# The experts' two layers as plain float32 products, the second one computed transposed and turned back

## The chip, the core and the metric

One core of one Trainium2 chip. The metric is device time in microseconds (us) from the start to the end of one launch of the kernel, median over several runs. PE is TensorE, DVE VectorE, ACT ScalarE, POOL GpSimd, SP the engine that issues most DMAs.

## What is computed

Three layers follow one another: a masked attention, a dense two-layer MLP with squared ReLU, and a mixture of eight experts. Only the last is touched:

```
def _moe2_ref(x, w_gate, w1, w2):          # N, D, E, F = 1536, 512, 8, 1024
    cap = N // E                           # 192 tokens for each expert
    logits = x @ w_gate
    order = np.argsort(-flat)              # best (token, expert) pairs first
    ...
    for e in range(E):
        mask = assigned == e
        h = np.maximum(x[mask] @ w1[e], 0.0)
        out[mask] = h @ w2[e]
```

In the part left out, the pairs are taken in this order, and a token goes to the first expert that still has room. Inputs and output are float32. The experts' weights are 8 x 2 x 512 x 1024 numbers, 33.5 MB.

## The kernel before

The whole program is written as operations with an engine, an estimated duration, a priority and dependencies; a planner (`Sched`) simulates the engines with these estimates, and the instructions are emitted in the order that comes out. So each engine's queue has a fixed order, and a wait in it holds up all that stands behind it. Buffers and PSUM banks are resources that an operation takes (`acq`) and gives back (`rel`). PSUM has two double banks (`S0`, `S1`) and four single ones (`TP0`, `TP1`, `m`, `O`, together called "B").

Attention and the MLP come first. Then the router and the experts run side by side. The **router** finds which expert fills first, then the next, in eight phases; each is a long chain of small DVE operations with a few PE steps: comparisons of all tokens' values (L1345, one for each tile of 128 tokens, 12, then 9, then 6 tiles), counts by PE (L1352), a transposition and a minimum (L1397 to L1409), places of the chosen tokens (L1143, L1146, L1421), their slots (L1465, L1471, L1475). A phase gives an expert's number `ei` and the indices `ix` of its 192 tokens. The next phase needs the tokens that are left.

For each **expert** `p`, POOL gathers the 192 tokens by an indirect DMA (L1652), PE turns them (L1668, L1669), and ACT and DVE write them as two parts, high and low, each rounded to float32r (L1672, L1676). float32r is the type that PE takes in one pass, with fewer bits of the mantissa. The weights come in four groups `g` of 256 hidden features, 1 MB each (L1614, L1615, two DMAs of 512 KB). Each group is split as well: ACT writes the high parts (L1618, two instructions), POOL and in part DVE the low parts, raw minus high (L1622, two instructions; `DVE_LO` tells which are DVE's). There are four raw places and five split ones.

First layer: for each group, two halves `j` of 128 features, four chunks `c` of 128 inputs. One product with the high weights on high and low tokens (L1707, 384 columns), one with the low weights on the high tokens (L1708, 192 columns). ACT and DVE add the two sums, apply ReLU and split the result again (L1711, L1715, L1718, L1723). Second layer: tokens are the stationary operand, w2 the moving one with 512 columns; per group and half, three products for tokens 0 to 127 (L1752 to L1754) and two for the other 64 (L1757 or L1760, L1758). The sums over all groups stay in a double bank, then ACT and DVE copy them (L1782, L1785, L1788), and POOL scatters the rows to the output (L1793). The last expert's results lie in two single banks.

`keep` (L1079) fills gaps of PE with products of no use (L1082) until the first expert's first product.

## Time and profile before

| | us |
|---|---|
| median of three runs | 909.86 (907.74 to 917.37) |
| span of the profiled execution | 906.2 |
| PE, DVE, ACT, POOL busy | 787.5, 770.8, 505.1, 579.2 |
| bytes moved by DMA | 113.21 MB |

The span runs from the first to the last instruction of one execution; it lies 3.7 us under the median. Busy times are sums over the span. Idle time is put down to the releaser, the instruction whose end let the engine go on. PE records are pipelined: a record's duration contains the way through the array, so the rate of a series is read from the distance of the starts. PEclk is the clock granted to the array (1 is full speed). In a timeline row the first number is the start in us, the second the duration, and `xN` says that N records of one kind stand in it.

### The profile page before, as it was taken

The page shows a single profiled execution, that of the slowest core. Times are in us where ns is not written, and L with a number is a line of the kernel's source. Part 1 is how long each engine was busy: PE and PEld are TensorE (multiplying, and loading weights), DVE is VectorE, ACT ScalarE, POOL GpSimd, SP SyncE. Part 2 cuts the span into 40 slices and gives each one's busy share as a digit, 9 for nine tenths or more (in the row PEclk, how much of TensorE's full clock was granted, in tenths as well). Part 3 has the DMA queues.
Part 4 walks back from the last instruction along what each step waited for, and adds up shares of the span by engine and source line. Part 5 has one row for each costly group of instructions (what it writes and reads, how often), then busy time and mean ns, then how long its engine had stood idle before and what let it go on. Part 6 is the DMA issues. An engine that isn't in the chain of part 4 may idle for free. (4 is left out here: it accounts for less than half of the span.)

```text
span 906.2 us, 14120 instructions
## 1 busy us (share of the span) xinstructions
PE 787.5 (87%) x4879; PEld 667.4 (74%) x4879; DVE 770.8 (85%) x1288; ACT 505.1 (56%) x943; POOL 579.2 (64%) x468
## 2 busy tenths in 40 slices
PE   8999999999779989989787876997787685888977
PEld 5797889889668878877676765984667474667866
DVE  6898999999987898998999998278898897986772
ACT  7898999999665535434433232454354343434642
POOL 3687787778775766755445454585566564567762
PEclk9999999999999999999899898988798796978999
DMA  8955856575122354333422220013442451645531
GB/s 201 234 127 125 180 128 143 120 162 125 47 94 97 137 185 140 129 117 125 163 93 94 91 94 1 12 60 107 144 157 75 147 177 60 214 149 169 204 134 35
DMA packets 99878, 113.21 MB, mean 125 GB/s; under 512 B 42560, under 2 KB 75712, under 8 KB 99808
## 3 DMA queue, kind: packets, MB, share of 16 engines
q1 hardware_dynamic: 97760, 106.03, 40.5%
q0 software_dynamic: 2048, 6.29, 2.1%
q8 instruction: 38, 0.62, 0.3%
q14 instruction: 32, 0.26, 0.1%
HBM read 82.42 MB, written 6.29 MB: 98 GB/s over the span
## 5 line engine op out<-in xcount | busy, mean ns | idle before, releaser
L1622 POOL TENSOR_TENSOR rf<-ff,rf 128x1024 fp32r<-128x1024 f32 x54 | 132.1, 2466 | 53.7 <-ACT rf L1618 53.4
L575 POOL TENSOR_TENSOR f<-f 128x768 f32<-128x768 f32 x96 | 144.8, 1512 | 32.0 <-PE psTP L583 13.2
L796 POOL TENSOR_TENSOR r<-f,r 128x384 fp32r<-128x384 f32 x64 | 85.7, 1341 | 99.1 <-ACT r L794 98.9
L773 POOL TENSOR_TENSOR r<-f,r 128x1024 fp32r<-128x1024 f32 x32 | 92.7, 2896 | 30.3 <-ACT r L771 25.7
L810 PE MATMUL psS<-r 128*128 128x512 f32 x384 | 100.2, 405 | 5.6 <-DVE f L820 4.6
L794 ACT ACTIVATE r<-f 128x384 fp32r<-128x384 f32 x64 | 33.3, 524 | 125.7 <-DVE f L792 125.7
L1707 PE MATMUL psS<-rf,rf 128*128 128x384 f32 x256 | 91.0, 409 | 10.8 <-DVE ff L1715 8.4
L563 DVE TENSOR_REDUCE f<-psS 128x1 f32<-128x768 f32 x96 | 90.5, 945 | 4.7 <-PE psS L547 3.1
L566 ACT ACTIVATE f<-psS,f 128x768 f32<-128x768 f32 x96 | 86.9, 906 | 3.9 <-POOL f L575 1.8
L547 PE MATMUL psS<-r 128*128 128x384 f32 x384 | 87.9, 350 | 0.8 <-ACT f L566 0.8
L810 PEld LDWEIGHTS psS<-r 128*128 128x128 f32 x384 | 73.3, 194 | 19.8 <-DVE f L820 4.9
L783 PE MATMUL psO<-r 128*128 128x384 f32 x408 | 80.5, 344 | 7.3 <-DVE f L792 7.3
L783 PE MATMUL psTP<-r 128*128 128x384 f32 x336 | 67.4, 349 | 19.0 <-DVE f L792 18.7
L783 PEld LDWEIGHTS psO<-r 128*128 128x128 f32 x408 | 73.1, 193 | 11.2 <-DVE f L792 10.7
L783 PEld LDWEIGHTS psTP<-r 128*128 128x128 f32 x336 | 59.9, 193 | 26.3 <-DVE f L792 24.9
L1618 ACT ACTIVATE rf<-ff 128x1024 fp32r<-128x1024 f32 x64 | 65.8, 1047 | 10.7 <-issue 9.4
L547 PEld LDWEIGHTS psS<-r 128*128 128x128 f32 x384 | 65.5, 190 | 4.7 <-ACT f L566 1.8
L1708 PE MATMUL psS<-rf,rf 128*128 128x192 f32 x256 | 68.9, 269 | 0.0
L1707 PEld LDWEIGHTS psS<-rf,rf 128*128 128x128 f32 x256 | 54.8, 214 | 13.0 <-DVE ff L1715 9.1
L758 DVE SCALAR_TENSOR_TENSOR f<-f 128x1024 int32<-128x1024 int32 x31 | 61.0, 1968 | 0.5
L1723 DVE SCALAR_TENSOR_TENSOR rf<-ff,rf 128x256 fp32r<-128x256 f32 x64 | 49.3, 812 | 9.8 <-ACT rf L1718 9.2
L873 DVE SCALAR_TENSOR_TENSOR f<-f,f 128x512 f32<-128x512 f32 x48 | 57.1, 1201 | 0.0
(398 smaller groups left out, 2074.4 us busy)
## 6 DMA issues: line engine op xcount, KB each, us to landing
ff<-in_moe_w_dram SPq DMA_DIRECT2D x64, 512.0 KB
r<-r SPq DMA_DIRECT2D x90, 192.0 KB
f<-in_moe_w_in_dram SPq DMA_DIRECT2D x32, 512.0 KB
f<-in_moe_w_out_dram SPq DMA_DIRECT2D x32, 512.0 KB
r<-r SPq DMA_DIRECT2D x15, 384.0 KB
f<-in_q_dram SPq DMA_DIRECT2D x8, 384.0 KB
f<-in_k_dram SPq DMA_DIRECT2D x8, 384.0 KB
f<-in_v_dram SPq DMA_DIRECT2D x8, 384.0 KB
```

Source lines behind the costliest of these rows:

```text
L547: nc.tensor.matmul(sbank(u)[:, hf, 0:384], T["q", (pr, h)][:, n, 128 * i:128 * i + 128], T["k", (pr, h)][:, n, 384 * hf:384 * hf + 384], s ...
L563: nc.vector.tensor_reduce(col(0, u), sbank(u)[:, :, 0:384], axis=AX.XY, op=OP.max, negate=True)
L566: nc.scalar.activation(P(u).rearrange("p (a b) -> p a b", a=2), sbank(u)[:, :, 0:384], AF.Exp, bias=col(0, u), accum_out=col(1, u))
L575: nc.gpsimd.tensor_tensor(Pn(u), P(u), col(3, u).to_broadcast([128, 768]), op=OP.mult)
L773: (nc.vector if s < EARLY_DVE else nc.gpsimd).tensor_tensor(lo, F, hi.bitcast(F32), op=OP.subtract)
L783: nc.tensor.matmul(hbank(s, hf), w[:, c], y[:, x, sl], start=(c == 0 and i == 0), stop=(c == 3 and i == 2))
L796: nc.gpsimd.tensor_tensor(hl[:, sl], r, hh[:, sl].bitcast(F32), op=OP.subtract)
L810: nc.tensor.matmul(abank(i), a[:, t], w, start=(f == 0 and j == 0), stop=(f == 15 and j == 2))
L1618: nc.scalar.activation(spl(p, g)[0][:, i], raw(p, g)[:, i], AF.Copy)
L1622: eng.tensor_tensor(l[:, i], raw(p, g)[:, i], h[:, i].bitcast(F32), op=OP.subtract)
L1707: nc.tensor.matmul(t[:, 0:384], h[:, f], x[:, c], start=(c == 0), stop=False)
L1708: nc.tensor.matmul(t[:, 192:384], l[:, f], x[:, c, 0:192], start=False, stop=(c == 3))
```

## The change

The experts' operands are no longer split. The weights are used as they come from the DMA, in float32; L1618 and L1622 are gone, and there are fifteen places for raw groups instead of four. The tokens are copied once after the turn, half by ACT, half by DVE. First layer: one float32 product of 192 columns for each `j` and `c`; then one ReLU from PSUM, by ACT for even groups, by DVE for odd ones. Second layer: w2 is now the stationary operand, four blocks `d` of 128 output features, and the 192 hidden columns are moving, so that the result comes out as features x tokens; eight products per group. The accumulators are first set to 0 by two bf16 products per expert. After the last group ACT and DVE copy the result, eight transpositions turn it back into PSUM, ACT and DVE copy it once more, and POOL scatters as before. PSUM: `S0` is held from the start of the stage and its two banks serve the first layer in turn; `S1` serves the second. The planner's estimates and priorities for these operations are new; the router's are not. The other lines of the diff only take comments out.

```diff
...
-DVE_LO = (0, 0, 0, 1, 2, 1, 2, 4)  # first parts of each expert's weights whose low half is made on the vector engine
-FP = {"h0": 23, "l0": 24.5, "p0": 1, "h1": -8.5, "p1": 28.5, "ga": 27, "xp": -0.5, "xh": -35.5, "xl": 13, "m1": 24.5, "hb": -38, "hs": -44.5, "hh": 51.5, "hl": 35.5, "m2": 70.5, "yb": 21, "ys": -13.5, "yo": -40.5, "sc": -10.5}
...
+FP = {"ga": 27, "xp": -0.5, "xe": -35.5, "m1": 24.5, "re": -38, "m2": 70.5, "ye": -30, "yt": -20, "yo": -40.5, "sc": -10.5}
...
-RF = (16, 16, 16, 16, 16, 6, 6, 3, 3, 3)
...
+RF = (8,) * 11 + (3, 3, 1.5, 1.5, 1.5, 1.5)
...
-UNITS_F = {"spl": (4000, 4016, 4032, 4048, 4064), "xT": (4080, 4086), "hf": (4092, 4095, 4098),
-           "raw": (5000, 5008, 5016, 5024), "xg": (5032, 5036), "hs": (5040, 5043), "yb": (5046, 5048), "yo": (5050, 5052, 5054, 5056)}
+UNITS_F = {"raw": (*(4000 + 8 * i for i in range(11)), 5000, 5008, 5016, 5024), "yT": (4088, 4091), "hx": (4094, 4095.5, 4097, 4098.5),
+           "xg": (5032, 5036), "xT": (5040, 5043), "yo": (5046, 5048, 5050, 5052, 5054, 5056), "A": ()}
+MMF = .346
...
-        def hi(i):
-            nc.scalar.activation(spl(p, g)[0][:, i], raw(p, g)[:, i], AF.Copy)
-
-        def lo(i, eng):
-            h, l = spl(p, g)
-            eng.tensor_tensor(l[:, i], raw(p, g)[:, i], h[:, i].bitcast(F32), op=OP.subtract)
...
         T["ld", p, g] = s = S.add("SP", .1, load, [T["v", p, v]], prio=p, acq="raw")
-        d = S.add("DMA", 2.9, None, [s], prio=p, lat=1.8)
-        T["h0", p, g] = h0 = S.add("ACT", .95, lambda: hi(0), [d], prio=FP["h0"], acq="spl")
-        if g < DVE_LO[p]:
-            l0 = S.add("DVE", 1.15, lambda: lo(0, nc.vector), [h0], prio=FP["l0"])
-        else:
-            l0 = S.add("POOL", 2.31, lambda: lo(0, nc.gpsimd), [h0], prio=FP["p0"])
-        h1 = S.add("ACT", .95, lambda: hi(1), [d, h0], prio=FP["h1"])
-        l1 = S.add("POOL", 2.31, lambda: lo(1, nc.gpsimd), [h1, l0], prio=FP["p1"], rel=[("raw", s)])
-        WD[p, g] = h0, l0, h1, l1
+        WD[p, g] = S.add("DMA", 4.6, None, [s], prio=p, lat=1.8)
...
     def xT(p):
-        return mem(unit(("xt", p, 0), "xT"), [4, 384], R)
+        return mem(unit(("xt", p, 0), "xT"), [4, 192])
...
-        def xt_hi(q):
-            nc.scalar.activation(xT(p)[:, 2 * q:2 * q + 2, 0:192], tv(q), AF.Copy)
-
...
+        def xt_ev(q):
+            o = xT(p)[:, 2 * q:2 * q + 2]
+            if q == 0:
+                nc.scalar.activation(o, tv(q), AF.Copy)
+            else:
+                nc.vector.tensor_copy(o, tv(q))
...
-            b = S.add("ACT", .38, lambda q=q: xt_hi(q), [a], prio=FP["xh"])
-            c = S.add("DVE", .47, lambda q=q: xt_lo(q), [a, b], prio=FP["xl"], rel=[("B", a)])
-            xd += [b, c]
+            T["xt", p, q] = a = S.add("PE", .44, lambda q=q: xt_pe(q), [gd, a], prio=FP["xp"], acq=("B",) if q else ("B", "xT"), rel=[("xg", ga)] if q else (), w=.6)
+            xd.append(S.add("DVE" if q else "ACT", .45 if q else .49, lambda q=q: xt_ev(q), [a], prio=FP["xe"], rel=[("B", a)]))
...
     def hf(n):
-        return mem(unit(("hf", n), "hf"), [2, 384], R)
+        return mem(unit(("h", n), "hx"), [2, 192])
+
+    def abank(n):
+        return ps(unit("hold", "S"))[:, unit(("A", n), "A")][:, 0:384].rearrange("p (j t) -> p j t", j=2)
...
         def mm(j, c):
...
-            nc.tensor.matmul(t[:, 0:384], h[:, f], x[:, c], start=(c == 0), stop=False)
-            nc.tensor.matmul(t[:, 192:384], l[:, f], x[:, c, 0:192], start=False, stop=(c == 3))
...
+            nc.tensor.matmul(abank(n)[:, j], raw(p, g)[:, 0, 256 * c + 128 * j:256 * c + 128 * j + 128], xT(p)[:, c], start=(c == 0), stop=(c == 3))
+
+        def relu():
+            if g % 2:
+                nc.vector.tensor_scalar(hf(n), abank(n), 0.0, None, op0=OP.max)
+            else:
+                nc.scalar.activation(hf(n), abank(n), AF.Relu)
...
-                a = S.add("PE", .268, lambda j=j, c=c: mm(j, c), [h0, l0, *xds[p][c // 2 * 2:c // 2 * 2 + 2], a], prio=FP["m1"], acq="S" if a is None else (), w=.8,
+                a = S.add("PE", MMF, lambda j=j, c=c: mm(j, c), [WD[p, g], xds[p][c // 2], a], prio=FP["m1"], acq="A" if a is None else (),
...
-        T["hs", n] = b = S.add("ACT", .38, h_b, [a], prio=FP["hb"], acq="hs")
...
+        T["h", n] = S.add("DVE" if g % 2 else "ACT", .5, relu, [a], prio=FP["re"], acq="hx", rel=[("A", T["A", n])])
+
+    def y(p):
+        return ps(unit(("y", p), "S"))[:, :, 0:384].rearrange("p b (d t) -> p b d t", d=2)
...
+        def mm(j, d):
+            nc.tensor.matmul(y(p)[:, d // 2, d % 2], raw(p, g)[:, 1, 512 * j + 128 * d:512 * j + 128 * d + 128], hf(n)[:, j], start=False, stop=((g, j, d % 2) == (3, 1, 1)))
+
+        def zero():
+            for b in range(2):
+                nc.tensor.matmul(ps(unit(("y", p), "S"))[:, b, 0:384], router.zero, router.zero[:, 0:1].to_broadcast([128, 384]), start=True, stop=False)
...
+        if g == 0:
+            T["y", p] = a = S.add("PE", .34, zero, [WD[p, g], T["h", n], a], prio=FP["m2"], acq="S")
+        for j, d in [(j, d) for j in range(2) for d in range(4)] if g < 3 else [(j, d) for b in (0, 2) for j in range(2) for d in (b, b + 1)]:
+            last = (j, d) == (1, 3)
+            a = S.add("PE", MMF, lambda j=j, d=d: mm(j, d), [WD[p, g], T["h", n], a], prio=FP["m2"],
+                      rel=[("raw", T["ld", p, g]), ("hx", T["h", n])] if last else ())
+            T["l2", p, d] = a
...
+        def yT():
+            return mem(unit(("ye", p), "yT"), [4, 192])
+
+        def y_ev(b):
+            o, i = yT()[:, 2 * b:2 * b + 2], y(p)[:, b]
+            if b == 0:
+                nc.scalar.activation(o, i, AF.Copy)
+            else:
+                nc.vector.tensor_copy(o, i)
+
+        def bank(h):
+            return ps(unit(("yt", p, h), "B"))[0:(128, 64)[h]]
+
+        def yt(h, b):
+            for d in (2 * b, 2 * b + 1):
+                nc.tensor.transpose(bank(h)[:, 128 * d:128 * d + 128], yT()[:, d, (0, 128)[h]:(128, 192)[h]], ident)
...
+        def yo_ev(h):
+            if h == 0:
+                nc.scalar.activation(yo(h), bank(h), AF.Copy)
+            else:
+                nc.vector.tensor_copy(yo(h), bank(h))
...
-        l2 = [T["l2", p, t if p == 7 else 0] for t in range(2)]
-        T["yb", p] = b = S.add("ACT", .52, y_b, [l2[1]], prio=FP["yb"], acq="yb")
-        T["yo", p, 1] = c = S.add("DVE", .6, y_s, [b], prio=FP["ys"], acq="yo", rel=[("yb", b)])
-        T["yo", p, 0] = d = S.add("ACT", .52, y_o, [l2[0]], prio=FP["yo"], acq="yo")
-        if p < 7:
-            S.add("NONE", 0.0, None, [c, d], rel=[("S", T["y", p])])
+        ev = []
+        for b in range(2):
+            a = S.add("DVE" if b else "ACT", .5, lambda b=b: y_ev(b), [T["l2", p, 2 * b], T["l2", p, 2 * b + 1]], prio=FP["ye"], acq=() if b else "yT")
+            if b == 0:
+                T["ye", p] = a
+            ev.append(a)
+        S.add("NONE", 0.0, None, ev, rel=[("S", T["y", p])])
...
+                tr[h, b] = a = S.add("PE", .22, lambda h=h, b=b: yt(h, b), [ev[b], tr.get((h, 0)), T["ye", p]], prio=FP["yt"], acq=() if b else "B", w=.6)
+                if b == 0:
+                    T["yt", p, h] = a
+        S.add("NONE", 0.0, None, [tr[0, 1], tr[1, 1]], rel=[("yT", T["ye", p])])
...
-            e = (d, c)[h]
+            T["yo", p, h] = e = S.add("ACT" if h == 0 else "DVE", .6, lambda h=h: yo_ev(h), [tr[h, 1]], prio=FP["yo"], acq="yo", rel=[("B", T["yt", p, h])])
...
+    T["hold"] = S.add("NONE", 0.0, None, L, prio=-1000, acq="S", rel=[("A", (0,)), ("A", (1,))])
...
```

How this moves the queues, at three places. Names like `psS_61` or `rf_5307` are buffers: psS the double banks, psTP, psm and psO the single ones, rf and ff places in SBUF.

PE, first expert, around the step with which the second router phase finds its minimum (L1397, L1403). Before:

```order
L1707 MATMUL psS_61<-rf_5312,rf_5307 128x384
L1708 MATMUL psS_61<-rf_5312,rf_5307 128x192
L1397 MATMUL psm<-ident,X 8x128
L1403 MATMUL psm<-ident,xm 128x8
L1707 MATMUL psS_60<-rf_5312,rf_5308 128x384
```

Now:

```order
L1677 MATMUL psS_61<-ff_5333,rf_5307 128x192 x3
L1677 MATMUL psS_61<-ff_5333,rf_5308 128x192
L1397 MATMUL psm<-ident,X 8x128
L1677 MATMUL psS_61<-ff_5333,rf_5308 128x192 x2
L1403 MATMUL psm<-ident,xm 128x8
L1677 MATMUL psS_61<-ff_5333,rf_5308 128x192 x5
```

The router's steps now stand between single float32 products; the products come from raw places (rf_5307 is the first group, rf_5308 the second).

POOL, from the second gather to the first expert's scatter. Before:

```order
L1652 DMA ff_5325<-x2d,ix 128x512
L1652 DMA ff_5325<-x2d,ix 64x512
L1657 COPY ei<-ei 128x1
L1622 TENSOR_TENSOR rf_5311<-ff_5320,rf_5311 128x1024
L1622 TENSOR_TENSOR rf_5310<-ff_5323,rf_5310 128x1024
L1622 TENSOR_TENSOR rf_5311<-ff_5320,rf_5311 128x1024
L1622 TENSOR_TENSOR rf_5307<-ff_5321,rf_5307 128x1024 x2
L1622 TENSOR_TENSOR rf_5308<-ff_5322,rf_5308 128x1024
L1792 MEMSET pad 128x1
L1793 DMA out_dram<-ff_5331,ix 1536x512
```

Now, the last rows ahead of that scatter, with the fourth gather:

```order
L1632 DMA ff_5332<-x2d,ix 128x512
L1632 DMA ff_5332<-x2d,ix 64x512
L1637 COPY ei<-ei 128x1
L1749 MEMSET pad 128x1
L1750 DMA out_dram<-ff_5336,ix 1536x512
```

POOL has nothing but gathers and scatters left, and the gathers of the third and fourth expert stand ahead of the first scatter.

PE, the end of the program, last products and what follows them. Before:

```order
L1758 MATMUL psTP_62<-rf_5308,rf_5315 64x512
L1760 MATMUL psTP_62<-rf_5308,rf_5315 128x512
L1752 MATMUL psm<-rf_5307,rf_5314 128x512
L1753 MATMUL psm<-rf_5307,rf_5314 128x512
L1754 MATMUL psm<-rf_5307,rf_5314 128x512
```

Now:

```order
L1702 MATMUL psS_60<-rf_5322,rf_5307 128x192 x8
L1702 MATMUL psS_60<-rf_5323,rf_5308 128x192 x7
L1736 MATMUL psTP_63<-ident,rf_5319 128x128 x2
L1736 MATMUL psTP_62<-ident,rf_5319 64x128 x2
L1702 MATMUL psS_60<-rf_5323,rf_5308 128x192
L1736 MATMUL psTP_63<-ident,rf_5319 128x128 x2
L1736 MATMUL psTP_62<-ident,rf_5319 64x128 x2
```

The second half of the transpositions stands behind the last product, with a copy by DVE between them.

More of the change, by code (lines that the diff above doesn't have):

```diff
@@ L1604, in raw @@
         return mem(unit(("ld", p, g), "raw"), [2, 1024])
-    def spl(p, g):
-        u = unit(("h0", p, g), "spl")
-        return mem(u, [2, 1024], R), mem(u + 8, [2, 1024], R)
     def weights(p, g, v):
@@ L1732, in add1 @@
-        T["hs", n] = b = S.add("ACT", .38, h_b, [a], prio=FP["hb"], acq="hs")
-        c = S.add("DVE", .47, h_s, [b], prio=FP["hs"], rel=[("S", T["SA", n])])
-        T["hf", n] = d = S.add("ACT", .38, h_hi, [c], prio=FP["hh"], acq="hf")
-        e = S.add("DVE", .54, h_lo, [d], prio=FP["hl"], rel=[("hs", b)])
-        T["hd", n] = [d, e]
-    def y(p, t):
-        return ps(unit(("y", p), "S"))[:, t] if p < 7 else ps(unit(("y", p, t), "B"))
+                    T["A", n] = a
+        T["h", n] = S.add("DVE" if g % 2 else "ACT", .5, relu, [a], prio=FP["re"], acq="hx", rel=[("A", T["A", n])])
@@ L1741, in add2 @@
+    def y(p):
+        return ps(unit(("y", p), "S"))[:, :, 0:384].rearrange("p b (d t) -> p b d t", d=2)
     def add2(p, g):
-        h0, l0, h1, l1 = WD[p, g]
         n = 4 * p + g
-        def mm(j, t):
-            h, l = (w[:, 1, 512 * j:512 * j + 512] for w in spl(p, g))
-            x = hf(n)[:, j]
-            o = y(p, t)
-            a, z = (g, j) == (0, 0), (g, j) == (3, 1)
-            if t == 0:
-                nc.tensor.matmul(o, x[:, 0:128], h, start=a, stop=False)
-                nc.tensor.matmul(o, x[:, 0:128], l, start=False, stop=False)
-                nc.tensor.matmul(o, x[:, 256:384], h, start=False, stop=z)
-            else:
-                if a:
-                    nc.tensor.matmul(o, x[:, 128:256], h, start=True, stop=False)
-                nc.tensor.matmul(o[0:64], x[:, 128:192], l, start=False, stop=False)
-                if not a:
-                    nc.tensor.matmul(o, x[:, 128:256], h, start=False, stop=z)
@@ L1762, in add2 @@
-        a = T.get(("l2d", n - 1))
-        for j, t in ((0, 0), (0, 1), (1, 1), (1, 0)) if g < 3 else ((0, 1), (1, 1), (0, 0), (1, 0)):
-            first = g == j == 0 and (p == 7 or t == 0)
-            last = (j, t) == (1, 0)
-            a = S.add("PE", (.648, .432)[t], lambda j=j, t=t: mm(j, t), [h1, l1, *T["hd", n], T.get(("l2", p, t)) if p == 7 else a], prio=FP["m2"] + (L7 if p == 7 and t == 0 else 0), acq=() if not first else "S" if p < 7 else "B",
-                      rel=[("spl", T["h0", p, g]), ("hf", T["hf", n])] if last and p < 7 else ())
-            if first:
-                T["y", p] = T["y", p, t] = a
-            T["l2", p, t] = a
+        def mm(j, d):
+            nc.tensor.matmul(y(p)[:, d // 2, d % 2], raw(p, g)[:, 1, 512 * j + 128 * d:512 * j + 128 * d + 128], hf(n)[:, j], start=False, stop=((g, j, d % 2) == (3, 1, 1)))
@@ L1771, in add2 @@
         T["l2d", n] = a
-        if p == 7:
-            S.add("NONE", 0.0, None, [T["l2", p, 0], T["l2", p, 1]], rel=[("spl", T["h0", p, g]), ("hf", T["hf", n])])
     def after(p):
         RT = RTs[p]
+        def yT():
[6 more added lines that the diff above has]
+                nc.vector.tensor_copy(o, i)
@@ L1787, in y_o @@
-        def y_o():
-            nc.scalar.activation(yo(0), y(p, 0), AF.Copy)
+        def yo_ev(h):
[3 more added lines that the diff above has]
+                nc.vector.tensor_copy(yo(h), bank(h))
         def scat(h):
@@ L1811, in experts @@
     add1(0, 0)
-    router.keep(S, ps, front, T["SA", 0])
+    router.keep(S, ps, front, T["A", 0])
     for p in range(8):
```

34 lines of the change are left out of this document (3 added, 31 removed).

## The prediction, made before the changed kernel ran

> **What bounds the kernel now.** I read the page's busy times first, then a table of stages, then single rows of the timeline.
>
> ```profile
> PE 787.5 (87%) x4879; PEld 667.4 (74%) x4879; DVE 770.8 (85%) x1288; ACT 505.1 (56%) x943; POOL 579.2 (64%) x468
> ```
>
> PE and DVE look alike over the span. The stages tell more. Columns are PE, PEld, DVE, ACT and POOL busy, granted clock, DMA share, GB/s.
>
> ```profile
> 0.00:612.00 612.00, 554.07 (x3164) 479.61 (x3164) 537.78 (x821) 377.57 (x758) 403.97 (x352) 0.97 0.44 119
> 612.00:640.00 28.00, 22.99 (x281) 15.16 (x282) 23.95 (x52) 12.47 (x13) 17.88 (x14) 0.74 0.48 156
> 640.00:845.00 205.00, 160.84 (x1180) 130.76 (x1180) 173.55 (x378) 87.25 (x131) 122.25 (x79) 0.86 0.42 138
> 845.00:890.00 45.00, 39.43 (x208) 33.78 (x208) 32.52 (x33) 24.88 (x37) 32.09 (x22) 0.96 0.44 151
> ```
>
> The change touches only what lies behind 612 us, 294 us of the 906.2. From 640 to 845 us the busiest engine is DVE (173.6 of 205), and PE runs at a clock of 0.86: it waits often enough to lose speed. What makes DVE busy is partly not work. The same instruction on 128 x 8 numbers (L1407) took 0.23 us in the first router phase and 4.13 us in the third, while POOL worked on two low halves of weights:
>
> ```profile
> 617.37 0.23 DVE L1407 SCALAR_TENSOR_TENSOR sc<-sc,th,rck 128x8 f32<-128x8 f32 x1
> 688.04 4.13 DVE L1407 SCALAR_TENSOR_TENSOR sc<-sc,th,rck 128x8 f32<-128x8 f32 x1
> 687.45 4.69 POOL L1622 TENSOR_TENSOR rf<-ff,rf 128x1024 fp32r<-128x1024 f32 x2
> 867.42 8.30 DVE L1622 TENSOR_TENSOR rf<-ff,rf 128x1024 fp32r<-128x1024 f32 x1 [0.49 <-ACT rf L1618]
> ```
>
> POOL's end of that row, 692.14, is DVE's end within 0.03 us. The last row, late in the program, is one DVE subtraction of 8.3 us. So the splitting holds up the experts directly and the router through DVE.
>
> ```profile
> L1622 POOL TENSOR_TENSOR rf<-ff,rf 128x1024 fp32r<-128x1024 f32 x54 | 132.1, 2466 | 53.7 <-ACT rf L1618 53.4
> L1618 ACT ACTIVATE rf<-ff 128x1024 fp32r<-128x1024 f32 x64 | 65.8, 1047 | 10.7 <-issue 9.4
> L1723 DVE SCALAR_TENSOR_TENSOR rf<-ff,rf 128x256 fp32r<-128x256 f32 x64 | 49.3, 812 | 9.8 <-ACT rf L1718 9.2
> ```
>
> **What is removed.** These three groups go: 132.1 us of POOL, 65.8 of ACT, 49.3 of DVE, with the smaller ones beside them. POOL keeps gathers and scatters. What comes in for them is 40 instructions on each of ACT and DVE (16 ReLUs and 24 copies out of PSUM), of 0.5 to 0.7 us by rows quoted below (L1672, L1785), some 24 us beside PE's products. If DVE and POOL cease to bound, PE is next, and the sum is made for PE.
>
> **The price of a float32 product.** Before, the pair L1707 and L1708 (384 + 192 columns) repeats every 0.28 us at full clock and a 512-column product every 0.23 us; at half clock the pair takes 0.54 us:
>
> ```profile
> 728.68 0.36 PE L1707 MATMUL psS<-rf,rf 128*128 128x384 f32 x1
> 728.96 0.36 PE L1707 MATMUL psS<-rf,rf 128*128 128x384 f32 x1
> 745.09 0.40 PE L1754 MATMUL psS<-rf,rf 128*128 128x512 f32 x1
> 745.33 0.39 PE L1752 MATMUL psS<-rf,rf 128*128 128x512 f32 x1
> 637.28 0.57 PE L1707 MATMUL psS<-rf,rf 128*128 128x384 f32 x1
> 637.82 0.57 PE L1707 MATMUL psS<-rf,rf 128*128 128x384 f32 x1
> ```
>
> That is 0.417 ns for a column and some 0.018 us beside it for each product. Per group 8 x 0.285 + 10 x 0.231 = 4.6 us, for 32 groups 147 us at full clock.
>
> Plain float32 products stand at two places of the trace, both small:
>
> ```profile
> 1.35 2.50 PE L403 MATMUL psTP<-ident 128*128 128x128 f32 x10 [1.35 <-POOL ident masks.py:199]
> 4.98 0.85 PE L324 MATMUL psm<-ident,f 128*128 128x128 f32 x3
> 6.00 0.49 PE L324 MATMUL psTP<-ident,f 128*128 128x128 f32 x3
> 589.90 0.95 PE L842 MATMUL psTP<-f,f 128*128 128x8 f32 x8
> ```
>
> L403 issues five products and L842 four, and they leave ten and eight records: a float32 product is two passes, each with a weight load of its own. L842 streams 8 columns only, so its spacing, (0.95 - 0.26) / 7 = 0.10 us, is the price of a weight load. L403 streams 128 columns and shows (2.50 - 0.42) / 9 = 0.231 us for a pass. It runs at half clock: the transpositions right behind it (L324) go from a spacing of 0.21 us to 0.11 us within a microsecond. At full clock a pass of 128 columns is thus 0.115 us, weight load included, which shows that the load lies beside the stream. For 192 columns there are two ends. Either the load was the limit in L403, and a pass stays at 0.115 us: 0.23 us for a product. Or the stream was, at two column times for each column, since each pass takes both parts of the moving number: 192 x 2 x 0.417 ns + 0.018 = 0.178 us, 0.356 us for a product. More is excluded, since L403 would have been slower. I take 0.356: L403 scaled by its columns gives nearly the same, 2 x 0.173, and the old kernel needed three float32r products for what is now one. 512 products are then **182 us**, between 118 and 187.
>
> The Trainium skill, "FP8 and Floating Point Precision", section TensorE Precision Notes, says that true float32 takes four passes, high and low of one operand with high and low of the other. By it a product of 192 columns is four streams of a float32r one, 0.32 us and the loads' rest, as in my choice; taking the trace's two records as the number of streams would give 0.23. No run here yet streams enough columns to show it.
>
> So PE's product work grows by 35 us at full clock. What pays for it is that PE no longer waits.
>
> **The other work of PE behind 632 us.** The router's steps are unchanged. Their busy times, in the order L1352, L1314, L1146, L1471, L1560:
>
> ```profile
> 632.00:906.20 274.20, 13.83 (x325) 10.92 (x321) 0.87 0.42 141
> 632.00:906.20 274.20, 6.29 (x36) 4.41 (x36) 0.87 0.42 141
> 632.00:906.20 274.20, 4.14 (x114) 3.56 (x114) 0.87 0.42 141
> 632.00:906.20 274.20, 4.02 (x54) 3.54 (x54) 0.87 0.42 141
> 632.00:906.20 274.20, 3.14 (x21) 2.55 (x21) 0.87 0.42 141
> 742.33 0.27 PE L1668 MATMUL psm<-ident,ff 128*128 128x128 f32 x1
> 743.91 0.27 PE L1669 MATMUL psTP<-ident,ff 64*128 64x64 f32 x1
> ```
>
> 31.4 us, of which about a quarter is the overlapping end of records and half clock; with the small steps I count 25 us. Turning an expert's tokens takes 1.78 us (from 742.33 to the start behind 743.91), for the seven later experts 12.5 us. New are 64 transpositions of results at L324's 0.11 us, 7 us, and 16 zero products of 384 columns, 0.18 us each, 3 us. Together **48 us**, between 40 and 60.
>
> **Start, waits, end.** The first expert's first tokens are copied at 631.8; its first product came only at 636.1, behind DVE's half of the split. Now two products need the first copy alone: start at **632.3**.
>
> ```profile
> 631.80 0.49 ACT L1672 ACTIVATE rf<-psm 128x384 fp32r<-128x384 f32 x1 [1.64 <-PE psm L1669]
> 636.11 0.69 PE L1707 MATMUL psS<-rf,rf 128*128 128x384 f32 x1
> 632.00:640.00 8.00, 6.57 (x73) 5.41 (x70) 6.65 (x6) 2.90 (x4) 6.88 (x3) 0.61 1.02 345
> ```
>
> The clock is down there (0.61), so the first products cost **3 us** more. The same row shows DMA at 345 GB/s: all 33.5 MB are 97 us at that rate, and with fifteen places the loads run ahead of 182 us of products; I cost them at nothing. If only four places' worth ran ahead, a group would still land every 3 us against 5.7 us of its products.
>
> PE's queue is fixed: behind a router step that waits for DVE stand the next products, and behind those the next router step. By the order, 42 products stand ahead of the turn of the second expert's tokens, and again 42 to the third's, 28 to the fourth's: 15, 15 and 10 us plus the steps between. The first phase took 9 us from its counts to its indices while POOL split nothing, and a comparison of 12 tiles takes 1.0 us, of 9 tiles then some 0.8:
>
> ```profile
> 614.45 0.17 DVE L1388 TENSOR_SCALAR full<-psS 128x8 f32<-128x8 f32 x1 [1.46 <-PE psS L1256]
> 623.45 0.15 DVE L1475 CAST ix<-psTP 128x2 int32<-128x2 f32 x1
> 622.52 1.01 DVE L1345 TENSOR_SCALAR ff<-ff,mx 128x1536 bf16<-128x1536 f32 x1
> ```
>
> So a phase of some 17 us is about as long as PE's work between; the waits are small, about one us a phase. I take **8 us**; nothing at best, 30 at worst, since PE waited for the router's DVE steps like this (in all, times, longest):
>
> ```profile
> PE psO L1352 <- DVE ff L1345: 5.9, 4, 2.5
> PE psm L1352 <- DVE ff L1345: 5.4, 1, 5.4
> ```
>
> At the end one copy and a set of transpositions come in:
>
> ```profile
> 898.76 0.68 DVE L1785 TENSOR_TENSOR ff<-psTP,ff 64x512 f32<-64x512 f32 x1 [2.64 <-ACT ff L1782]
> 899.74 0.39 PE L1754 MATMUL psm<-rf,rf 128*128 128x512 f32 x1
> 901.04 0.97 POOL L1793 DMA_INDIRECT out_dram<-ff,ix  x1 [0.31 <-ACT ff L1788]
> ```
>
> Before, the last product ended at 900.1 and the span 6.1 us later. An added copy (0.5 to 0.7), transpositions (0.7) and two more hand-overs of some 0.3 us make it **9 us**.
>
> Sum: 632.3 + 182 + 48 + 3 + 8 + 9 = 882 us of span, 24 less than 906.2. The profiled span is 3.7 us under the median of the runs; with the same distance the time is 886 us.
>
> **Rivals.**
>
> *The router starves PE at half clock (slower).* PE's queue has short router steps between long products, and each wait of about a clock window turns the array to half speed. For it: the clock of 0.86 from 640 to 845, with the same order of dependencies. Against it: DVE has lost its contention with POOL, and products now fill the gaps. Price: the 194 products that stand ahead of the router's last step run at 0.61 as from 632 to 640: 194 x 0.356 x (1 / 0.61 - 1) = 44 us, so 930 us. It decides from 24 us on, 67 products at half speed.
>
> *The router's waits stay as before (no change).* If the chain's length is its dependencies and not POOL's hold on DVE, some 20 us more of waits come between the products, and the time is 906 us. Against it: the 0.23 and 4.13 us of L1407.
>
> *A pass is limited by the weight load (much faster).* Then products are 118 us, PE is no longer the bound, and the router's seven phases at 17 to 25 us and the last expert set the end: about 840 us. For it speaks that L403 fits both readings.
>
> **How the numbers follow.** My forecast has 0.67, with a range of 870 to 900 from the bounds of the other work and the waits; unchanged waits 0.12; half clock 0.13; load-limited passes 0.08. About 1% is what a measurement of this kernel tells from no change: faster needs less than 900.8. So faster 0.75, same 0.12, slower 0.13. The range of 8 in 10 leaves out most of the fast rival and the dearer half of the slow one: 858 to 918.
>
> **What would show it right or wrong.** Records of L1677 start 0.18 us apart at full clock; DVE's L1407 at 0.2 us in every phase; granted clock above 0.95 from 660 us on; PE busy without a gap over 1 us behind the seventh router phase; gathers 17 to 25 us apart. Wrong it is if L1677 passes come at 0.115 us, if PE waits more than 30 us for DVE or DMA behind 632 us, or if the clock lies under 0.9.

## The result and the profile after

| | kernel before | changed kernel |
|---|---|---|
| time, median of the runs | 909.84 us (907.74 to 917.37, 4 runs) | 879.48 us (878.4 to 881.21, 4 runs) |
| profiled execution: time, span | 909.86, 906.2 us | 881.21, 879.4 us |
| mean granted clock | 0.938 | 0.97 |

The ratio of the times is 0.9658, with a 95% interval of 0.9612 to 0.9705: the changed kernel is faster by 30 us. The forecast was 886, so 6.5 us too high, and the terms of its sum were off by more than that, in both directions.

The stages of the changed kernel, with the columns of the prediction's table (PE, PEld, DVE, ACT and POOL busy, granted clock, DMA share, GB/s):

```profile
612.00:640.00 28.00, 22.58 (x272) 14.86 (x273) 19.94 (x54) 9.74 (x12) 10.28 (x11) 0.68 0.41 130
640.00:845.00 205.00, 197.15 (x1577) 181.11 (x1577) 85.02 (x322) 28.11 (x52) 29.95 (x46) 0.99 0.51 174
845.00:870.00 25.00, 22.67 (x139) 21.68 (x139) 2.26 (x4) 2.07 (x4) 2.10 (x4) 1.00 0.05 16
870.00:879.40 9.40, 1.67 (x12) 1.09 (x10) 1.24 (x2) 0.60 (x1) 1.98 (x3) 0.77 0.13 42
```

From 640 to 845 us DVE's busy time has fallen from 173.6 to 85.0 us and POOL's from 122.3 to 30.0, while PE is busy for 197 of 205 us and its clock has gone from 0.86 to 0.99. Of these 88.5 us of DVE some are work that was removed, and some are work that was kept and now runs at its own length. These two router groups exist in both kernels; first before, then after, behind 612 us:

```profile
L1345 DVE TENSOR_SCALAR ff<-ff,mx 128x768 bf16<-128x768 f32 (+2 forms) x44 | 53.5, 1263 | 1.1 <-PE psO L1352 1.1
L1407 DVE SCALAR_TENSOR_TENSOR sc<-sc,th,rck 128x8 f32<-128x8 f32 x7 | 8.7, 1244 | 0.2
```

```profile
L1345 DVE TENSOR_SCALAR ff<-ff,mx 128x768 bf16<-128x768 f32 (+2 forms) x44 | 32.2, 780 | 1.3 <-ACT ff L1319 1.3
L1407 DVE SCALAR_TENSOR_TENSOR sc<-sc,th,rck 128x8 f32<-128x8 f32 x7 | 1.6, 227 | 0.3
```

The same 44 comparisons took 53.5 us and now take 32.2; the same seven small steps took 8.7 us and now 1.6. The router therefore moves faster. The tokens of the first and of the last expert are fetched, before and after, at:

```profile
624.57 1.96 POOL L1652 DMA_INDIRECT ff<-x2d,ix  x1 [8.70 <-ACT ff L1341]
...
831.39 1.00 POOL L1652 DMA_INDIRECT ff<-x2d,ix  x1
```

```profile
626.76 1.96 POOL L1632 DMA_INDIRECT ff<-x2d,ix  x1 [8.81 <-ACT ff L1341]
...
752.33 0.97 POOL L1632 DMA_INDIRECT ff<-x2d,ix  x1 [6.03 <-PE psTP L1649]
```

Seven phases went from 207 us to 126. Behind 752 us nothing is left but products, copies and transpositions; this part is 127 us long, and PE sets it.

The start of the first gather is a useful mark. Up to there every program of this study computes the same thing, yet among the profiled executions it lies anywhere between 623.4 and 630.3 us. In what follows "from the first gather" means the span minus this start: 281.6 us before, 252.6 us after. It leaves out a variation that has nothing to do with the experts.

### The profile page after: what moved, and what is told of

Same layout as the page of the kernel before. It is cut to its first block, busy times and chain, and to the rows that moved or that the text cites. A ratio compares the mean times of both kernels' runs of the same rounds, so it can differ in the third digit from the quotient of the medians.

```text
span 879.4 us, 14288 instructions
## 1 busy us (share of the span) xinstructions
PE 796.3 (91%) x5148; PEld 697.2 (79%) x5148; DVE 644.7 (73%) x1198; ACT 415.7 (47%) x823; POOL 446.8 (51%) x414
## 5 line engine op out<-in xcount | busy, mean ns | idle before, releaser
L783 PE MATMUL psTP<-r 128*128 128x384 f32 x336 | 65.4, 341 | 23.1 <-DVE f L792 22.8
L783 PE MATMUL psO<-r 128*128 128x384 f32 x408 | 78.3, 338 | 8.2 <-DVE f L792 8.2
L783 PEld LDWEIGHTS psTP<-r 128*128 128x128 f32 x336 | 58.0, 188 | 30.9 <-DVE f L792 29.6
L783 PEld LDWEIGHTS psO<-r 128*128 128x128 f32 x408 | 71.1, 188 | 11.9 <-DVE f L792 11.4
L1702 PE MATMUL psS<-rf,rf 128*128 128x192 f32 x384 | 74.4, 332 | 2.8 <-ACT rf L1727 2.8
L1677 PE MATMUL psS<-ff,rf 128*128 128x192 f32 x384 | 74.9, 341 | 1.4 <-ACT rf L1683 1.4
L1632 POOL DMA_INDIRECT ff<-x2d,ix x16 | 18.9, 1184 | 109.1 <-DVE ix L1475 70.0
L1750 POOL DMA_INDIRECT out_dram<-ff,ix x16 | 15.1, 947 | 110.1 <-DVE ff L1745 107.1
L1702 PEld LDWEIGHTS psS<-rf,rf 128*128 128x128 f32 x384 | 62.3, 190 | 4.8 <-ACT rf L1727 4.1
L1677 PEld LDWEIGHTS psS<-ff,rf 128*128 128x128 f32 x384 | 64.0, 196 | 2.5 <-ACT rf L1683 2.2
```

The lines of the kernel that those rows point to most:

```text
L783: nc.tensor.matmul(hbank(s, hf), w[:, c], y[:, x, sl], start=(c == 0 and i == 0), stop=(c == 3 and i == 2))
L1677: nc.tensor.matmul(abank(n)[:, j], raw(p, g)[:, 0, 256 * c + 128 * j:256 * c + 128 * j + 128], xT(p)[:, c], start=(c == 0), stop=(c == 3))
L1702: nc.tensor.matmul(y(p)[:, d // 2, d % 2], raw(p, g)[:, 1, 512 * j + 128 * d:512 * j + 128 * d + 128], hf(n)[:, j], start=False, stop=((g, ...
```

## The experiments

The theory: POOL's wide subtractions hold DVE's steps, DVE's steps hold the router, and the router holds the experts; once they are gone PE sets the time, with 0.33 us for a float32 product. The rivals: DVE was slow for reasons of its own; the gain comes from loading weights further ahead; the router's chain lies just under PE; a product's price is its weight loads. Later runs ask what about POOL's work does the harm, and whether splitting and speed can be had together.

### POOL's low halves left out of the kernel before

```diff
 def lo(i, eng):
+    if eng is nc.gpsimd:
+        return
     h, l = spl(p, g)
...
-            h, l = (w[:, 0] for w in spl(p, g))
+            h = l = spl(p, g)[0][:, 0]
```

The second layer likewise takes its high halves twice.

> The kernel before, with POOL's 54 low halves of the weights (132 us of POOL) left out and its products of low halves reading the high halves instead; the order on PE, DVE and ACT and the number of products stay. The theory (POOL's wide subtractions hold up DVE's small steps, and through them the router, and with it the experts): L1407 takes 0.23 us in every phase, DVE's own low halves near 1.2 us, and the time falls by 40 to 65 us, to about 855, below the changed kernel, since its products are 147 us of PE work against some 170. The rival (DVE is slow for a reason of its own, POOL does no harm): L1407 still shows 4 us, and the time stays within 10 us of 910. A second rival (ACT's high halves and the four copies that each group goes through keep the experts late): L1407 is quick, yet the time falls by less than 25 us.

Measured: 833.52 us, ratio 0.9168 (0.9127 to 0.921); 206.4 us from the first gather instead of 281.6. So 75 us of the old kernel hung on POOL's 54 subtractions, more than the 40 to 65 expected, and their removal alone ends 46 us below the changed kernel. These 75 hold two things at once, DVE's slow steps and the experts' own wait for the low halves; the next run shows the first of them alone, in the changed kernel. Its two groups of small steps, and its stages:

```profile
L1345 DVE TENSOR_SCALAR ff<-ff,mx 128x768 bf16<-128x768 f32 (+2 forms) x44 | 32.6, 786 | 2.7 <-PE psO L1352 1.8 <-ACT ff L1319 0.8
...
L1407 DVE SCALAR_TENSOR_TENSOR sc<-sc,th,rck 128x8 f32<-128x8 f32 x7 | 1.6, 227 | 0.3
```

```profile
640.00:763.00 123.00, 121.41 (x1091) 101.06 (x1091) 96.05 (x362) 77.01 (x116) 23.50 (x33) 1.00 0.63 210
763.00:832.00 69.00, 63.29 (x344) 53.93 (x343) 26.32 (x51) 37.25 (x56) 11.11 (x21) 1.00 0.44 149
```

L1407 is quick again and PE is busy all through, with ACT's 64 high halves and all the copies still there. Both rivals fall: ACT's share of the splitting was hidden, DVE had no slowness of its own. The change thus does two things: it saves some 75 us by emptying POOL and gives back some 46 by dearer products, transpositions and waits. What remains is its gain of 29. Of the 46, products are 20 (167 us, worked out below, against the prediction's 147), transpositions back and zero products up to 14 (busy 10.0 and 3.9 us in the changed kernel); the rest is waits, a longer end and what overlaps differently, and was not taken apart.

### POOL's load put back beside the changed kernel

```diff
 def relu():
+    for i in range((1 if g < NL[p] else 2) if p < 7 else 0):
+        t = mem(5024, [2, 1024])[:, i]
+        nc.gpsimd.tensor_tensor(t, t, t, op=OP.subtract)
```

> The changed kernel with 45 subtractions of 128x1024 float32 on POOL added, on memory that nobody else uses (one of the fifteen places of weights given up for it); nothing waits for them, only POOL's own gathers and scatters stand behind some. The theory (POOL's wide operations hold DVE): L1407 goes from 0.23 us to several us where it meets one, POOL's subtraction takes 2.3 us alone and more beside DVE, PE waits for DVE, and the time is 890 to 915. The rival (the contention was no part of it): L1407 stays at 0.23 us and the time within 4 us of 880, but for gathers that start late.

Measured: 916.62 us, 1.0054 of the kernel before (1.0028 to 1.008), 289.4 us from the first gather. (The subtractions came to 47, not 45.) Results that nobody reads cost 37 us, all of the change's gain. All of it falls ahead of the last gather, which comes 162.4 us after the first instead of 125.6: the loss lies where the router works. DVE and POOL at one such place:

```profile
718.51 8.04 DVE L1304 TENSOR_TENSOR PM<-PM,mx 128x48 f32<-128x48 f32 x1
```

```profile
719.04 7.44 POOL L1682 TENSOR_TENSOR ff<-ff 128x1024 f32<-128x1024 f32 x4
```

A DVE step on 48 numbers per partition, otherwise 0.22 us, ends at 726.55, within 0.1 us of the end of POOL's fourth subtraction in a row (726.48). It did not get its turn between them. The gathers were not late by POOL's queue: POOL stood idle before the later ones, waiting for DVE (12.9 us before the second, 25.8 before the third).

### Loading no further ahead

```diff
-UNITS_F = {"raw": (*(4000 + 8 * i for i in range(11)), 5000, 5008, 5016, 5024), ...
+UNITS_F = {"raw": (5000, 5008, 5016, 5024), ...
```

> The changed kernel with four places for raw weights in place of fifteen. The theory (PE bounds, a group takes it 5.2 us, and a load lands 5.1 us after its issue, so two groups ahead are enough): 879 to 886 us. The rival (the gain of the change is that weights are now loaded far ahead): PE waits for DMA at the heads of groups, and 895 us or more.

Measured: 879.49 us, ratio 0.9655 (0.9625 to 0.9686); 252.9 us from the first gather. Eleven places of 8 KB in each partition make no difference to the time that can be seen, and the rival falls. The planner made another order for it, in which the last gather comes 138.9 us after the first, 13 later than in the changed kernel; the end is the same all the same.

### Half the columns in the second layer

```diff
-nc.tensor.matmul(y(p)[:, d // 2, d % 2], raw(...)[...], hf(n)[:, j], ...
+nc.tensor.matmul(y(p)[:, d // 2, d % 2, 0:96], raw(...)[...], hf(n)[:, j, 0:96], ...
```

> The changed kernel with the second layer's 256 products over the first 96 of the 192 tokens alone; the other half of the results stays zero. The order is the same. The theory (a float32 product of 192 columns costs two passes of 0.163 us, set by the stream, and PE bounds the stage): a record of L1702 shrinks to 0.08 us, or to about 0.10 if the weight load is the floor there (0.10 us by L842); 512 records save 32 to 43 us, and the time falls nearly as much, to 837 to 850. The rival (the weight load already sets 0.163 us): the records stay at 0.16 us and the time at 880. A second rival (the router's chain lies just under PE): the records shrink, but the time falls by less than 15 us, and PE waits instead.

Measured: 860.56 us, ratio 0.9447 (0.9402 to 0.9492); 230.2 us from the first gather, 22.4 less; by the medians it is 18.9 less. That is short of the theory's 32 to 43 and more than the second rival's 15. Records of the two layers in its trace:

```profile
787.71 1.80 PE L1702 MATMUL psS<-rf,rf 128*128 128x96 f32 x14
789.57 2.87 PE L1677 MATMUL psS<-ff,rf 128*128 128x192 f32 x16
```

A group's time holds one full record and the starts of the others. With 0.27 us for a single record of 96 columns the spacing is (1.80 - 0.27) / 13 = 0.118 us; with 0.33 for one of 192 it is (2.87 - 0.33) / 15 = 0.169. Two other groups give 0.109 and 0.163. Half the columns save less than a third, so at 96 columns something else than the number of columns sets the pace, at about 0.115 us. That fits the 0.10 to 0.115 us that the prediction read for a weight load; no run varies the load alone. At 192 columns the stream sets it: 0.163 us is 2.04 times 192 columns of 0.417 ns. 512 records at 0.048 us less are 25 us, of which 22.4 came off the time.

### The second layer's products left out

```diff
 def mm(j, d):
+    if (g, j, d % 2) != (3, 1, 1):
+        return
     nc.tensor.matmul(y(p)[:, d // 2, d % 2], ...
```

> The changed kernel with 240 of the second layer's 256 products left out (16 stay, which end the sums). The order of the rest is the same. The theory (PE bounds, a product is 0.33 us): the time falls by 65 to 78 us, to about 802 to 815, since the seven router phases of about 17 us and the last expert would end only at some 770. The rival (the router's chain lies just under PE): a fall of less than 45 us, 835 or more, with PE waiting for DVE.

Measured: 843.63 us, ratio 0.9279 (0.9217 to 0.9341), a fall of some 36 us (216.2 us from the first gather) for 480 records of 0.163 us, 78 us of work. The time came out as the rival said. Up to 752 us, and behind it, first this kernel and then the changed one:

```profile
640.00:752.00 112.00, 98.07 (x866) 84.02 (x865) 71.97 (x297) 18.75 (x34) 19.35 (x26) 0.82 0.67 226
752.00:840.00 88.00, 64.81 (x356) 55.13 (x355) 14.32 (x25) 11.42 (x22) 14.63 (x27) 0.93 0.34 117
```

```profile
640.00:752.00 112.00, 109.80 (x1050) 98.82 (x1049) 73.92 (x303) 19.35 (x35) 19.40 (x26) 0.99 0.69 236
752.00:871.00 119.00, 111.02 (x672) 104.66 (x671) 13.36 (x23) 10.83 (x21) 12.65 (x24) 1.00 0.24 81
```

The last gather starts at 752.28 us here and at 752.33 in the changed kernel: up to there the work left out brought nothing. With less to do PE did not get ahead. It stood idle for 13.9 us of the first row instead of 2.2, mostly for DVE and ACT, and its clock was 0.82 instead of 0.99, so that what remained took longer. Only behind the last gather does the work left out come off, 39 of some 50 us.

It does not follow that products cost nothing while the router works. From the second gather to the last the changed kernel takes 99.2 us and this one 103.6. With half the columns, some 8 us of products less there, it is 95.4; in the next experiment, with dearer products, it is 108.9. So in the changed kernel PE did set the pace here, and its listed waits from 640 to 752 us are 2.1 us, none of them for the router. But the router lies close behind: more work on PE costs time at once, less work brings half of it or nothing. How far the waits and how far the lower clock used up the gain was not taken apart.

### The second layer not transposed

```diff
-nc.tensor.matmul(y(p)[:, d // 2, d % 2], raw(p, g)[:, 1, 512 * j + 128 * d:...], hf(n)[:, j], ...
+nc.tensor.matmul(y(p, d), hf(n)[:, j, t], raw(p, g)[:, 1, 512 * j:512 * j + 512], ...
```

The zero products, the copies to yT and the transpositions back are gone in it; results are copied straight to the scatter.

> The changed kernel with the second layer not transposed: tokens stationary (128 and 64), weights moving in 512 columns, so four products for each group in place of eight, and no zero products, copies and transpositions of results. The theory (a float32 product costs 1.7 ns for each moving column): four products of 0.85 us against eight of 0.33, 0.8 us more for each of 32 groups, 26 us more; some 11 us of transpositions and zero products go and 1.5 us at the end: 890 to 898 us. The rival (a product costs mostly by its count, its weight loads): 865 us or less.

Measured: 908.77 us, ratio 0.9957 (0.993 to 0.9983), 280.5 us from the first gather, 28 more than with the transposed layer. The rival is excluded, and the theory's range ended 11 us too low:

```profile
789.31 2.13 PE L1703 MATMUL psS<-ff,rf 128*64 128x512 f32 x4
802.55 4.80 PE L1703 MATMUL psS<-rf,rf 128*128 128x512 f32 x10
```

With 0.59 us for a single record the spacing is (2.13 - 0.59) / 3 = 0.513 us in the first group and (4.80 - 0.59) / 9 = 0.468 in the second; over all groups of four records and more it is 0.48, or 0.94 ns for a column, where 192 columns cost 0.85. So the 128 products cost 256 x 0.48 = 123 us against 512 x 0.163 = 83, 40 more where the theory had 26, of which some 12 come back with the zero products and transpositions, as the theory had it. Nearly all of the change's gain needs the transposed layer: plain float32 without it brings 0.4%, in the order that the planner makes for it.

### The splitting moved to DVE, in the kernel before

```diff
-DVE_LO = (0, 0, 0, 1, 2, 1, 2, 4)
+DVE_LO = (4, 4, 4, 4, 4, 4, 4, 4)
...
-l1 = S.add("POOL", 2.31, lambda: lo(1, nc.gpsimd), [h1, l0], prio=FP["p1"], ...
+l1 = S.add("DVE", 1.15, lambda: lo(1, nc.vector), [h1, l0], prio=FP["l0"], ...
```

> The kernel before with all 64 low halves of the weights made by DVE, none by POOL (the planner knows of it and orders anew). The theory (POOL's wide subtractions are the harm, not the splitting as such; 147 us of products against 170): without them DVE's low half takes 1.24 us, 54 more of them are 67 us more of DVE, which then has some 208 us of work in 220: DVE bounds, 855 to 885 us, and it may beat the changed kernel's 879. The rival (the splitting costs the same wherever it is done): 900 or more.

Measured: 879.0 us, ratio 0.9647 (0.9547 to 0.9746), 247.6 us from the first gather. The harm was POOL's, not the splitting's: with 67 us more on DVE, and none on POOL, the old products end where plain float32 does. The planner knew of the move and made another order, which may have its share in this; the interval is wide.

```profile
L1622 DVE TENSOR_TENSOR rf<-ff,rf 128x1024 fp32r<-128x1024 f32 x64 | 77.2, 1221 | 5.5 <-ACT rf L1618 5.3
```

### POOL's low halves in four pieces

```diff
-eng.tensor_tensor(l[:, i], raw(p, g)[:, i], h[:, i].bitcast(F32), op=OP.subtract)
+for z in range(0, 1024, 1024 if eng is nc.vector else 256):
+    c = slice(z, z + (1024 if eng is nc.vector else 256))
+    eng.tensor_tensor(l[:, i, c], raw(p, g)[:, i, c], h[:, i, c].bitcast(F32), op=OP.subtract)
```

> The kernel before with each of POOL's low halves made in four pieces of 128x256 in place of one of 128x1024. In the changed kernel with added POOL work one DVE step of 128x48 took 8.04 us, through four POOL subtractions in a row (719.04 to 726.48). The theory (DVE does not get its turn between POOL's instructions while they follow on one another): the pieces change little, 905 to 925 us, and L1407 still shows several us. The rival (DVE waits for the instruction that is under way, and no longer): no small DVE step is over some 0.9 us, and the time falls to 875 to 895.

Measured: 903.78 us, ratio 0.9898 (0.9812 to 0.9985), 275.7 us from the first gather. The time lies just under the theory's 905 to 925 and far from the rival's 875 to 895. Smaller pieces relieve a little (L1407 falls to 308 ns on average, against the theory's "still several us"), though POOL's pieces add up to 162.6 us where the whole ones took 132.1. But the mechanism of the theory shows in the largest row of DVE, and below it POOL's:

```profile
746.00 14.46 DVE L1345 TENSOR_SCALAR ff<-ff,mx 128x768 bf16<-128x768 f32 x1
```

```profile
746.34 13.70 POOL L1624 TENSOR_TENSOR rf<-ff,rf 128x256 fp32r<-128x256 f32 x20
```

One comparison that takes 0.6 us elsewhere waited through twenty pieces, to 760.46; POOL's last piece ended at 760.04.

### Writing without reading

```diff
-nc.gpsimd.tensor_tensor(t, t, t, op=OP.subtract)
+nc.gpsimd.memset(mem(5024, [2, 1024]), 0.0)
```

> The changed kernel with 45 memsets of 128x2048 float32 on POOL where the earlier run had 45 subtractions of 128x1024; one takes 1.80 us, nearly as long as the subtraction's 1.9, but it reads nothing. The theory (what holds DVE is POOL's reading, since it is DVE's steps with two inputs in SBUF that were long): L1304 and L1407 stay at 0.23 us and the time within 6 us of 880. The rival (any wide POOL instruction holds DVE, or the gathers behind them are late): 900 or more.

Measured: 907.94 us, ratio 0.9966 (0.9929 to 1.0004), 277.7 us from the first gather, 25 more than in the changed kernel, with 47 memsets. POOL again stood idle before most gathers, waiting for DVE's indices (67.8 us in all). The steps named by the theory stayed short and the time rose all the same:

```profile
L1345 DVE TENSOR_SCALAR ff<-ff,mx 128x768 bf16<-128x768 f32 (+2 forms) x44 | 53.1, 1254 | 0.6 <-ACT ff L1319 0.6
...
L1399 DVE TENSOR_SCALAR full<-full 128x8 f32<-128x8 f32 x7 | 4.1, 590 | 0.0
...
L1407 DVE SCALAR_TENSOR_TENSOR sc<-sc,th,rck 128x8 f32<-128x8 f32 x7 | 1.6, 227 | 0.3
...
L1304 DVE TENSOR_TENSOR PM<-PM,mx 128x48 f32<-128x48 f32 (+2 forms) x6 | 1.3, 221 | 0.1
```

A memset holds DVE's steps with one tensor input from SBUF (L1345: 1254 ns for 780; L1399: 590 for 179) and leaves alone those with two (L1407, L1304); the subtraction held both kinds (L1345: 1005 ns, L1304: 1525). L1345 alone, in its 44 steps, takes 20.9 us more than in the changed kernel. So the theory was half right: it named the wrong steps as the ones that matter. The Trainium skill, "SBUF — State Buffer", section Who interferes with whom, draws the same line: a DVE instruction with two SBUF inputs contends with a GpSimd instruction that reads SBUF, one in two-port mode with any. No run here shows which mode L1345 and L1399 were in. The section also says that whoever issues first holds the shared ports for the whole instruction; here the loser waited through four instructions and through twenty in a row.

### Splitting again, only where DVE is idle

The last four experts of the changed kernel get the old second layer: weights and hidden values split by ACT and DVE (POOL splits nothing), three float32r products, tokens stationary. A second kernel does so for the last five, and a third for the last four, with more places for what is split.

```diff
+P0 = 4
...
+        if p >= P0:
+            T["h2", p, g] = h = S.add("ACT", .95, lambda: nc.scalar.activation(spl(p, g)[0], raw(p, g)[:, 1], AF.Copy), ...
+            T["l2w", p, g] = S.add("DVE", 1.2, lambda: nc.vector.tensor_tensor(spl(p, g)[1], raw(p, g)[:, 1], ...
```

> The changed kernel, but the experts that come fifth to eighth have the second layer's weights and hidden values split on ACT and DVE again (POOL splits nothing), with the products as in the kernel before: tokens stationary, three float32r products in place of plain float32, no transpositions back. In those experts DVE is idle (12 of 116 us behind 755 us of the changed kernel) and PE bounds. The theory (PE bounds there): per expert 32 products of 0.326 us give way to 40 of 0.231, 1.2 us less, and the zero products and transpositions back go, some 1.7 us with the waits at them; 3 us for each of four experts, and 2 us at the end: 862 to 870 us. The rival (the splits on DVE and ACT bring their waits back): 876 or more.

> The same from the fourth expert on, whose products fall into the last router phases. The theory: 1 to 3 us less than with four experts, since the router's chain sets the pace there, or the same. The rival: DVE's four further low halves, 1.24 us each, stand between the router's steps and it is 2 us or more slower than with four.

Measured: 873.9 us, ratio 0.9568 (0.9524 to 0.9612), with the last four; 875.12, ratio 0.9587 (0.954 to 0.9633), with the last five. From the first gather 245.6 and 246.9 us, against 252.6. The first is 5.6 us under the changed kernel, with all its runs below the changed kernel's (871.18 to 876.46 against 878.40 to 881.21). The second's 4.4 us are not decided, since its runs reach up to 879.94, and between the two nothing is decided either. The expected gain was 9 to 17 us. PE's waits in the kernel with the last four split, from 740 us on (in all, times, longest):

```profile
PE psS L1688 <- DVE rf L1693: 4.7, 6, 0.8
PE psS L1688 <- ACT rf L1709: 3.9, 6, 0.7
PE psS L1688 <- issue: 1.4, 1, 1.4
```

Ten microseconds of waits, mostly for ReLU and low half, have come in at the first layer, where the changed kernel lists none from 740 us on. This is what the rival named, but it explains only a part: in all, PE's listed waits from 740 us on are 12.6 us here and 8.8 in the changed kernel, since some hand-overs at the second layer's end have gone.

Then the places for hidden values were doubled, with four places for split weights instead of three and nine for raw ones instead of eleven.

> The kernel with the last four experts' second layer split, with four places instead of two for the hidden values' high and low halves, four instead of three for the split weights, and nine instead of eleven for raw weights; the order of the products at the end is the same. In the run before, PE waited 10 us for ReLU and low halves of the hidden values, which themselves waited for their place (ACT's L1709 at 818.96 was released by PE's L1735, a reader of the place). The theory (the places are the cause): these waits fall to under 3 us and the time by 5 to 9 us, to 864 to 870. The rival (the waits come from the time that ReLU and the low half take one after the other): no change within 2 us.

```diff
-"spl": (4056, 4064, 4072), "hf": (4080, 4083), ...
+"spl": (4040, 4048, 4056, 4064), "hf": (4072, 4075, 4078, 4081), ...
```

Measured: 876.49 us, ratio 0.9608 (0.9565 to 0.9652), 249.7 us from the first gather; the same two waits stand at 4.7 and 3.8 us. So the number of places was not the cause. The time is 2.6 us more than before the doubling, where the rival expected no change within 2. Which dependency it is stays open: ACT's ReLU still starts six times behind a product of the second layer (L1735), and why was not found.

## Why the prediction was right

Its mechanism is shown by the first two experiments: take POOL's 54 subtractions away from the old kernel and 75 us go; put 47 into the new one, where nothing waits for their results, and 37 come back. That the number came so near is in part luck, since errors of 15 us one way and of some 13 the other met in the sum. By its own steps:

**The price of a product** was the largest term, and was mis-sized. A group at full clock and one at the start:

```profile
652.98 2.11 PE L1677 MATMUL psS<-ff,rf 128*128 128x192 f32 x12
```

```profile
636.81 1.63 PE L1677 MATMUL psS<-ff,rf 128*128 128x192 f32 x4
```

(2.11 - 0.33) / 11 = 0.162 us for a record, two of them for a product. The prediction's 0.178 added 0.018 us for each pass to two column times for each column; of that addition nothing is to be seen. 512 products are 167 us instead of 182, which is 15 of excess. The choice between the two ends was right: 96 columns fell to the weight load's 0.115 us, 192 did not. At 192 columns 0.326 us is 4.07 streams of 0.417 ns a column, so the two records cost as much as four streams, which agrees with the Trainium skill, "FP8 and Floating Point Precision", section TensorE Precision Notes. At 512 columns a product costs 0.96 us, 4.5 such streams, so the rule does not give every width.

**The start** was put at 632.3 and came at 636.8:

```profile
631.71 0.27 PE L1648 MATMUL psm<-ident,ff 128*128 128x128 f32 x1
633.74 0.37 PE L1649 MATMUL psm<-ident,ff 64*128 64x64 f32 x1 [1.76 <-DMA ff<-x2d,ix]
```

About two of the 4.5 us are the variation ahead of the first gather (626.76 against 624.57). The rest is that the second gather's tokens landed only at 633.7, and that the turn behind them ran at half clock, with the second half of the tokens (to 636.5) in PE's order ahead of the first product. That two products need only the first copy is true and did not help.

**The cold clock**, 3 us: the first records came 0.326 us apart, twice 0.163. The four groups up to 645 us, 22 records, take 6.7 us from each group's start to the next record behind it, where 22 x 0.163 is 3.6; that is 3.1 us more. Right.

**Other work and waits**, 48 and 8 us: from 636.8 to the last product's end at 871.0 are 234.2 us; less 167 and 3.1 that is 64.1. Of these PE stands idle for 10.2 (it is busy for 224.0), so 54 are left for the other work, within its bounds; they are a remainder and were not measured by themselves. The waits have the size but not the place that the prediction gave them:

```profile
PE psS L1702 <- ACT rf L1727: 4.0, 7, 0.6
PE psm L1736 <- DVE rf L1729: 3.3, 4, 1.1
PE psTP L1736 <- DVE rf L1729: 1.8, 2, 1.1
```

Behind the first product all listed waits (columns as before: in all, times, longest; with 1.7 us of L1677 for ACT's ReLU) are for copies out of PSUM, most of them new with the change; the router, for which the 8 us were meant, costs none there. The sign "no gap over 1 us" failed by these waits of 1.1 us.

**The end**, 9 us behind the last product:

```profile
870.52 0.49 PE L1702 MATMUL psS<-rf,rf 128*128 128x192 f32 x2
871.12 0.56 DVE L1729 COPY rf<-psS 128x384 f32<-128x384 f32 x1 [11.40 <-PE psS L1702]
871.73 0.66 PE L1736 MATMUL psTP<-ident,rf 128*128 128x128 f32 x4 [0.72 <-DVE rf L1729]
872.43 0.68 DVE L1745 COPY ff<-psTP 64x512 f32<-64x512 f32 x1 [0.75 <-PE psTP L1736]
874.59 0.97 POOL L1750 DMA_INDIRECT out_dram<-ff,ix  x1 [0.19 <-issue]
```

8.4 us from 871.0 to 879.4. Right.

With these sizes the sum is 636.8 + 167 + 54 + 3.1 + 10.2 + 8.4 = 879.5, against a span of 879.4. That it closes proves nothing, since the 54 are what was left over; against the prediction's terms the start is 4.5 us more, the products 15 less, the other work 6 more, the waits 2 more. Around the span lay 1.8 us, where the prediction added 3.7.

**What it reasoned too simply.** It took PE for the bound behind 632 us. That holds from 752 us on, where 39 of some 50 us of products left out came off, and before it only just: the router lies so close behind that half the columns brought about half of their 8 us between the second gather and the last, and leaving the second layer out brought nothing there. By this a longer router phase would have made the router the bound; no run tries it. The rival of the half clock, 0.13, did not occur here, but a run came near it: with the second layer left out PE's clock was 0.82 up to the last gather. Gathers were said to come 17 to 25 us apart; the first two came 26 apart, the last three 9 to 14.

## What to carry to other kernels

Work on POOL that nobody waits for is not free: the price is on DVE's rows, where a small step shows several microseconds, and it is found by comparing the same step in two places of one profile. In the two places shown a run of POOL instructions held DVE like a single one. And a busy engine is not proved to be the bound by its share. Leave out some of its work and add some, and see how far the marks behind it and the end move; leaving out very much brings waits and a lower clock of its own, and then the mark says little.

## What the runs showed of the hardware that was not expected

- One DVE instruction took 14.46 us instead of 0.6, through twenty POOL instructions of 0.7 us each, and got no turn between them.
- A memset, which reads nothing, lengthened L1345 from 780 to 1254 ns, and 47 of them cost 25 us from the first gather on; steps with two SBUF inputs stayed at 0.22 us.
- A pass of a float32 product costs about 0.115 us for 96 columns, 0.163 for 192 and 0.48 for 512: 1.2, 0.85 and 0.94 ns for a column. Why wide passes cost more than two column times is not explained by any run here.
- The part ahead of the first gather, the same work in every program, took from 623.4 to 630.3 us in the profiled executions.
